# A first MoE tile of 288 tokens instead of 256, with its third piece transposed at the end of attention

## The chip, the cores and the metric

The kernel runs on one core of a Trainium2 chip. The metric is the time of one execution on the device, in microseconds (us). The kernel before takes 747.06 us, the median of three runs (746.73 to 747.48).

The engines are TensorE (PE: matmul and transpose, with its weight loads as PEld), VectorE (DVE), ScalarE (ACT), GpSimd (POOL) and SyncE (SP, which issues DMAs). Each runs its own instructions in order; they meet through semaphores. PE writes into PSUM, from which DVE and ACT take the results away.

## The reference

Three layers on 4 batches of 576 tokens, all in fp32: attention with a threshold on the scores (8 heads of 64), a mixture of 8 experts (512 to 1024 and back) in which a token keeps the expert of the token before it when its local gate is at least one half, and a second mixture of 4 attention experts, two for each token.

```python
scores = scale * np.matmul(q, k.transpose(0, 1, 3, 2))
thresh = np.max(scores, axis=-1, keepdims=True) - tau
scores = np.where(scores >= thresh, scores, -1000000000.0)
attn = np.exp(scores - np.max(scores, axis=-1, keepdims=True))
...
for b in range(B):
    prev_e = -1
    for s in range(S):
        fresh_e = int(np.argmax(logits[b, s]))
        e = fresh_e if s == 0 or local_gate[b, s] < 0.5 else (prev_e if prev_e >= 0 else fresh_e)
        prev_e = e
        ...
        h = np.maximum(x[b, s] @ w1[e], 0.0)
        out[b, s] = p[e] * (h @ w2[e])
...
for e in range(E):          # second mixture: 4 experts, top 2
    ...
    ye = a @ v @ wo[e]
```

## The kernel before

Products in fp32 are made of a high and a low half: three matmuls (high by high, high by low, low by high) take the place of one. A "split" makes the halves: the high half is a rounded copy (usually on ACT), the low half the difference (on DVE or POOL).

**Attention** (`stage1`, to about 281 us) goes through 16 pairs of heads, p = 0 to 15, each with nine tiles of scores. A score tile S (L246 to L251) takes one of three PSUM buffers in a ring; DVE takes the row maxima (L257), ACT the exponentials (L267), DVE the thresholding (L280, which reads S again and so sets that buffer free), and PE transposes the result (L293, X) and multiplies by v (L336, Y). When a pair is finished its rows are transposed on PE (L371; for the last pair's first half into a buffer of the score ring, S), ACT copies them (xraw), DVE takes the reciprocal of the sums (L363, rc, from input that POOL collects, L357 to L360), and POOL normalises (L396). The order is written out by hand: the table `W` and the numbers beside it give each step a time in units of a score tile, and steps are put down in the order of these numbers. The queries and keys of the next pair are split meanwhile, low halves on POOL (L204, L209).

**Early routing** (`Route.early`) runs inside the last pairs, by the times in `EARLY`. It routes batches 0 to 2, finds the fullest expert, and gives each of its tokens a position: `ranks` (L665) and `place` (L700) bring rank and position to `sle`, and POOL turns them into a column and a place within it (`column`, L707 to L718). One-hot matrices `ln` (L723, six on POOL at a time, and on DVE) and a product (L731, `invert`) turn that into token lists `inv`, 128 tokens to a column.

**The MoE stage** cuts the tokens of an expert into tiles of two kinds: P with 256 tokens (2 columns of `inv`), and L with 352 (3 columns; the first L, number 0, has `NL0` = 288, two chunks of 128 and one of 32). `SEQ` is the order of the tiles. Tile 0 belongs to the fullest expert of batches 0 to 2. Its tokens are gathered during the last pair of attention (`rows0`, at time `R0`, an indirect DMA on POOL, L1778), transposed on PE into score buffers (`tx0`, L1797, at the times `TX0`, by `xt.spare`), and split into xTPh (ACT, L1802) and xTPl (DVE, L1803). The halves of its expert's weights are split in the same stretch (`split0`, at the times `S0`: L924 to L927).

The rest of routing (`Route.main`, about 284 to 318 us) needs the logits of the last pair, and is a chain of small steps across PE, ACT and DVE. Tile 0 fills PE meanwhile: `start` cuts its work into pieces (first layer `h_mm`, L1054, in PSUM banks "acc"; second layer `y_mm`, L1083, in banks "py"), `FILL` says how many pieces stand between two steps of routing, and the evacuation of a bank (`hT_ev`: relu on ACT, L1043, low half on DVE, L1046) is put into `M.late` and taken out at set places. After routing the pieces that are left stand ahead of and between the transposes of tile 1 (`tx`, L1012), by `LEFT`. From about 320 us the other tiles follow one another, first layer and second layer, and then the second mixture.

In a chunk of 64 tokens or fewer ("packed"), high and low half lie side by side in `hT`, so that one matmul takes both, and `y_ev` adds the two results.

## Time and profile before

| | before |
|---|---|
| time, median of 3 | 747.06 us (746.73 to 747.48) |
| profiled execution | 748.55 us |
| its span | 746.8 us |
| PE busy | 722.0 us, 97% |
| DVE busy | 544.8 us, 73% |
| ACT busy | 490.7 us, 66% |
| POOL busy | 285.6 us, 38% |

The rows come from one execution taken by the profiler. Its time stands beside its span, the time from its first to its last instruction. In a timeline row stand the start, the duration, the engine, the line of the program, the operation, out<-in by the program's names, their sizes and the count; in brackets, how long the engine was idle before it and what released it. Neighbouring instructions of one line stand in one row. Matmuls overlap, so the duration of a matmul is longer than its distance from the next.

### The profile page before, as it was taken

The numbers are of one execution on the slowest core, as the hardware profiler recorded it, in microseconds if no ns is written. First come the engines' busy times: TensorE is split into PE (matmuls) and PEld (weight loads), VectorE is DVE, ScalarE is ACT, GpSimd is POOL, SyncE is SP. The second block draws the span as 40 slices with busy tenths as digits, with TensorE's granted clock in tenths as the row PEclk, the third lists the DMA queues.
The fourth block names the chain that finished last, engine by engine and source line by source line (L and its number), as shares of the span: only waits on it lengthen the run. The fifth ranks groups of instructions, "written<-read, shape, count | busy, mean of one in ns | idle before, by whom it ended". The sixth has DMA issues, their size and how long they took to land.

```text
span 746.8 us, 14233 instructions
## 1 busy us (share of the span) xinstructions
PE 722.0 (97%) x5063; PEld 611.4 (82%) x5063; DVE 544.8 (73%) x1427; ACT 490.7 (66%) x1026; POOL 285.6 (38%) x442
## 2 busy tenths in 40 slices
PE   5999999999999998999999999999998999999996
PEld 4887887888887777798889899989788888888874
DVE  7998999899988987725574475554269888878780
ACT  5888887888887784224565465444256887777883
POOL 6888888878777891300110110000356000000000
PEclk9999999999999999999999999999999999999999
DMA  8439444443332430295755656601333000100103
GB/s 281 149 116 315 147 124 139 137 156 120 122 126 66 185 119 18 87 372 179 253 204 206 240 184 211 237 1 53 95 86 99 2 16 1 43 15 29 44 29 104
DMA packets 37409, 95.40 MB, mean 128 GB/s; under 512 B 4337, under 2 KB 14833, under 8 KB 33233
## 3 DMA queue, kind: packets, MB, share of 16 engines
q1 hardware_dynamic: 30960, 73.62, 28.7%
q0 software_dynamic: 5360, 19.34, 8.3%
q10 hardware_dynamic: 1008, 1.44, 0.6%
q8 instruction: 42, 0.69, 0.4%
q14 instruction: 39, 0.31, 0.1%
HBM read 75.58 MB, written 18.81 MB: 126 GB/s over the span
## 4 chain that ended last, share of the span: by engine, by line
PE 84%; DVE 7%; ACT 4%; DMA 2%; issue 1%; POOL 1%; ACTq 0%; DVEq 0%; POOLq 0%
PE py L1083 16%; PE acc L1054 15%; PE Y L336 10%; PE S L246 9%; PE X L293 8%; PE AV L1647 4%; PE X L1596 3%; PE Y L371 2%; PE S L251 2%; PE S L1526 1%; PE px L1012 1%; PE S L1527 1%; PE misc L1446 1%; PE misc L1678 1%; PE misc L1677 1%
## 5 line engine op out<-in xcount | busy, mean ns | idle before, releaser
L280 DVE SCALAR_TENSOR_TENSOR P<-S,nm,E 128x576 f32<-128x576 f32 x144 | 116.3, 815 | 10.2 <-ACT E L267 4.5
L257 DVE TENSOR_REDUCE nm<-S 128x1 f32<-128x576 f32 x144 | 105.9, 754 | 17.6 <-PE S L246 16.8
L1083 PE MATMUL py<-w2h,hT 128*128 128x512 f32 (+2 forms) x344 | 114.8, 400 | 0.0
L267 ACT ACTIVATE E<-S,nm 128x576 f32<-128x576 f32 x144 | 104.1, 747 | 7.1 <-DVE nm L257 6.5
L246 PE MATMUL S<-KK,QS 128*128 128x288 f32 x256 | 84.0, 343 | 7.3 <-DVE QS L219 5.3
L293 PE MATMUL X<-cst,P 128*128 128x128 f32 x576 | 87.1, 278 | 1.4 <-ACT PT L304 0.7
L1778 POOL DMA_INDIRECT xg<-x_dram,inv x22 | 23.6, 1074 | 163.8 <-PE px L1012 128.2
L293 PEld LDWEIGHTS X<-cst,P 128*128 128x128 f32 x576 | 67.0, 142 | 16.1 <-issue 7.5
L304 ACT ACTIVATE PT<-X 128x512 f32<-128x512 f32 x128 | 75.8, 605 | 3.9 <-PE X L293 1.1
L1054 PE MATMUL acc<-xTh,w1h 128*128 128x256 f32 (+2 forms) x256 | 76.4, 299 | 0.0
L1054 PE MATMUL acc<-xTl,w1h 128*128 128x256 f32 (+2 forms) x256 | 76.0, 297 | 0.0
L1054 PE MATMUL acc<-xTh,w1l 128*128 128x256 f32 (+2 forms) x256 | 75.9, 297 | 0.0
L1083 PEld LDWEIGHTS py<-w2h,hT 128*128 128x128 f32 (+2 forms) x344 | 63.0, 183 | 15.4
L246 PE MATMUL S<-KL,QS 128*128 128x288 f32 x256 | 73.3, 300 | 0.3 <-DVE KL L201 0.3
L1083 PE MATMUL py<-w2l,hT 128*128 128x512 f32 (+2 forms) x176 | 69.4, 394 | 0.0
L336 PE MATMUL Y<-PT,v 128*64 128x320 f32 (+1 forms) x512 | 69.1, 412 | 0.2 <-ACT G L604 0.2
L1046 DVE SCALAR_TENSOR_TENSOR hT<-acc,hT 128x352 fp32r<-128x352 f32 (+3 forms) x60 | 30.4, 519 | 44.9 <-ACT hT L1043 44.9
L1043 ACT ACTIVATE hT<-acc 128x352 fp32r<-128x352 f32 (+2 forms) x52 | 26.2, 508 | 55.6 <-PE acc L1054 51.7
L246 PEld LDWEIGHTS S<-KK,QS 128*128 128x128 f32 x256 | 49.6, 194 | 8.8 <-ACT KK L192 5.2
L336 PEld LDWEIGHTS Y<-PT,v 128*64 128x64 f32 x512 | 33.9, 136 | 24.4 <-issue 4.8
L1847 POOL DMA_INDIRECT raw<-yg,slot x18 | 17.6, 980 | 86.8 <-DMA yg<-y 62.0
L246 PEld LDWEIGHTS S<-KL,QS 128*128 128x128 f32 x256 | 49.9, 195 | 0.6 <-DVE KL L201 0.6
(397 smaller groups left out, 1921.4 us busy)
## 6 DMA issues: line engine op xcount, KB each, us to landing
raw<-in_w_dram SPq DMA_DIRECT2D x32, 1024.0 KB, 5.4
kraw<-in_kT_dram SPq DMA_DIRECT2D x15, 608.0 KB, 4.1
QS<-in_qT_dram POOLq DMA_DIRECT2D x15, 576.0 KB, 4.1
v<-in_vp_dram SPq DMA_DIRECT2D x16, 320.0 KB, 3.0
yg<-y SPq DMA_DIRECT2D x17, 256.0 KB, 4.9
qraw<-in_qx_dram SPq DMA_DIRECT2D x15, 288.0 KB, 2.8
x_dram<-xr SPq DMA_DIRECT2D x16, 256.0 KB, 2.4
yg<-raw SPq DMA_DIRECT2D x1, 3072.0 KB, 12.9
```

The costliest lines, as they stand in the source:

```text
L246: nc.tensor.matmul(o, QS[p % NQ][:, a, cs], k[i][:, sl(576 * a)], start=(n == 0), stop=(n == 1))
L257: nc.vector.tensor_reduce(nm[:, 0:1], t[:, :, :288], axis=AX.XY, op=ALU.min)
L267: nc.scalar.activation(e, t[:, :, :288], AF.Exp, scale=-1.0, bias=nm[:, 0:1])
L280: nc.vector.scalar_tensor_tensor(PP[p, c][:, S * a:S * a + S].rearrange("p (h n) -> p h n", h=2), t[:, :, :288], nm[:, 1:2], e, op0=ALU.is ...
L293: nc.tensor.transpose(x[:, 128 * kc:128 * kc + 128], pp[:, o:o + 128], ident)
L304: nc.scalar.activation(PT[p, h][:, a, :, f:f + 128], x.rearrange("p (k q) -> p k q", k=4), AF.Copy)
L336: nc.tensor.matmul(out, l, r, start=s, stop=e, skip_group_check=True)
L1043: nc.scalar.activation(h[..., 0:w], p, AF.Relu)
L1046: nc.vector.scalar_tensor_tensor(h[..., low(t, c)], p[..., c], 0.0, h[..., c].bitcast(F32), op0=ALU.max, op1=ALU.subtract)
L1054: nc.tensor.matmul(o, a[:, fs], x[:, k, 0:w], start=(first and n == 0), stop=(k == 3 and n == 2), skip_group_check=True)
L1083: nc.tensor.matmul(ys[t][u][0:m], hT[t][i][:, f, k], w[:, 512 * f:512 * f + 512], start=(i == 0 and f == 0 and n == 0), stop=(i == 3 and f ...
L1647: nc.tensor.matmul(o[half(a), f:NH[h]], l, r, start=(k == 0), stop=(k == (1, 4)[h]), skip_group_check=True)
```

## The change

- Tile 0 becomes the 288-token tile and tile 1 a 256-token tile (`SEQ`). `rows0` gathers three pieces, the third of 32 tokens in a buffer of `qraw`; there are three transposes `tx0`, the last with 32 rows.
- The times `TX0`, `recip` and `S0` change: the copies and subtractions of the transposed rows stand ahead of the last pair's reciprocal, and the split of the first w2 chunk behind it.
- `column` now holds the arithmetic on the ranks too, which stood in `ranks` before: a token whose position is 288 or more gets its column from its rank less 288 (`NL0`).
- `start` takes one bank for each 288 columns, four banks ("py", "py", "acc", "acc") in turn, in pieces of six matmuls; a packed chunk of tile 0 follows at the end. `FILL` and `LEFT` change with the number of pieces (36 instead of 32).
- `hT` keeps the low half at a fixed offset, and POOL copies the packed chunk's low half beside its high half.
- The list `inv` has the columns of tile 0 at its end (last three instead of first two), so `main` writes 31 columns instead of 32, and `n0` has a sixth value.

```diff
-            T = dict(W, row=(11.3, 14.36), rev=(11.7, 14.7), recip=10.6, tpm=(8.79, 11.25), pmev=(9.07, 11.66))
+            T = dict(W, row=(11.3, 14.36), rev=(11.7, 14.7), recip=11.69, tpm=(8.79, 11.25), pmev=(9.07, 11.66))
...
     def rows0():
-        return P1.tile([128, 2, DM], F32, name="xg0", tag="P", bufs=5)
+        t = P1.tile([128, 2, DM], F32, name="xg0", tag="P", bufs=5)
+        return t[:, 0], t[:, 1], P1.tile([128, S], F32, name="qraw", bufs=2)[0:NL0 - 256, 0:DM]
...
-            q, one = self.rq, 1.5 * 2.0 ** 23
-            gp.tensor_scalar(q, sl[:, 0], -63.5, 1.0 / 128.0, op0=ALU.add, op1=ALU.mult)
-            gp.tensor_scalar(q, q, one, 1.0, op0=ALU.add, op1=ALU.mult)
-            gp.tensor_scalar(q, q, -one, 1.0, op0=ALU.add, op1=ALU.mult)
-            gp.tensor_scalar(self.place, q, -128.0, 1.0, op0=ALU.mult, op1=ALU.mult)
-            gp.tensor_tensor(self.place, self.place, sl[:, 0], op=ALU.add)
...
-            v.tensor_scalar(self.n0[:, 0:1], ti[:, 1:2], 256.0, t[:, 2:3], op0=ALU.min, op1=ALU.mult)
-            v.tensor_scalar(self.n0[:, 1:2], t[:, 2:3], NL0 - float(NL), NL - 511.0, op0=ALU.mult, op1=ALU.add)
+            v.tensor_scalar(self.n0[:, 0:1], ti[:, 1:2], float(NL0), t[:, 2:3], op0=ALU.min, op1=ALU.mult)
+            v.tensor_scalar(self.n0[:, 1:2], t[:, 2:3], NP0 - float(NL), NL - 511.0, op0=ALU.mult, op1=ALU.add)
...
+            v.tensor_scalar(self.n0[:, 5:6], t[:, 2:3], 3.0 - NCOL, NCOL - 3.0, op0=ALU.mult, op1=ALU.add)
...
         def column(*_):
-            sl, rq = T["sl"][:, 1], self.rq
-            f = T["f"] = E.tile([128, 4, 5, B], F32, name="fe")
+            sl, q, place, one = T["sl"][:, 1], self.rq, self.place, 1.5 * 2.0 ** 23
+            f = T["f"] = X.tile([128, 5, 5, B], F32, name="fe")
+            g = f[:, 4]
+            for i in (3, 0, 1, 2):
+                gp.tensor_scalar(f[:, i], sl, float(min(128 * i, NL0)), 1.0, op0=ALU.is_ge, op1=ALU.mult)
+                if i == 3:
+                    gp.tensor_scalar(g, f[:, 3], -float(NL0), 1.0, op0=ALU.mult, op1=ALU.mult)
+                    gp.tensor_tensor(g, g, T["sl"][:, 0], op=ALU.add)
+                    gp.tensor_scalar(q, g, -63.5, 1.0 / 128.0, op0=ALU.add, op1=ALU.mult)
+                    gp.tensor_scalar(q, q, one, 1.0, op0=ALU.add, op1=ALU.mult)
+                    gp.tensor_scalar(q, q, -one, 1.0, op0=ALU.add, op1=ALU.mult)
+                    gp.tensor_scalar(place, q, -128.0, 1.0, op0=ALU.mult, op1=ALU.mult)
+                    gp.tensor_tensor(place, place, g, op=ALU.add)
+            r2 = T["r2"] = X.tile([128, 5, B, 3], F16, name="r2e")
             for i in range(3):
-                gp.tensor_scalar(f[:, i], sl, 128.0 * i, 1.0, op0=ALU.is_ge, op1=ALU.mult)
-            r2 = T["r2"] = E.tile([128, 5, B, 2], F16, name="r2e")
-            for i in range(2):
                 gp.tensor_tensor(r2[:, :, :, i], f[:, i], f[:, i + 1], op=ALU.subtract)
-            gp.tensor_scalar(f[:, 3], f[:, 0], -2.0, 1.0, op0=ALU.mult, op1=ALU.mult)
-            gp.tensor_tensor(rq, rq, f[:, 3], op=ALU.add)
-            gp.tensor_scalar(f[:, 3], rq, 0.0, -128.0, op0=ALU.is_lt, op1=ALU.mult)
-            gp.tensor_tensor(rq, rq, f[:, 3], op=ALU.add)
-
-            gp.tensor_scalar(f[:, 3], f[:, 2], -1.0, 1.0, op0=ALU.mult, op1=ALU.add)
-            gp.tensor_tensor(self.s0.rearrange("p (j b) -> p j b", b=B), sl, f[:, 3], op=ALU.mult)
+            gp.tensor_tensor(f[:, 0], f[:, 0], f[:, 3], op=ALU.subtract)
+            gp.tensor_scalar(g, f[:, 0], -128.0, 1.0, op0=ALU.mult, op1=ALU.mult)
+            gp.tensor_tensor(q, q, g, op=ALU.add)
+            gp.tensor_scalar(g, sl, 128.0 * (NCOL - 3), 1.0, op0=ALU.add, op1=ALU.mult)
+            gp.tensor_tensor(self.s0.rearrange("p (j b) -> p j b", b=B), g, f[:, 0], op=ALU.mult)
...
-                mm(pi[:, 0:2], self.ln[:, j, b], T["r2"][:, j, b], start=(k == 0), stop=(k == 14))
-            return lambda: v.tensor_scalar(self.inv[:, 0:2], pi[:, 0:2], MID, None, op0=ALU.add)
-
-        return [copies, *self.choose_steps(slice(0, 3), gp), rows("A", 1), rows("G", 0), rest, flat, scan(0), scan(1), counted, turn,
+                mm(pi[:, 0:3], self.ln[:, j, b], T["r2"][:, j, b], start=(k == 0), stop=(k == 14))
+            return lambda: v.tensor_scalar(self.inv[:, NCOL - 3:], pi[:, 0:3], MID, None, op0=ALU.add)
...
-        NC = NCOL - 2
+        NC = NCOL - 3
...
-SEQ = [("P", 0), ("L", 0), ("P", 1), ("P", 2), ("L", 1), ("P", 3), ("P", 4), ("L", 2), ("L", 3)]
+SEQ = [("L", 0), ("P", 0), ("P", 1), ("P", 2), ("L", 1), ("P", 3), ("P", 4), ("L", 2), ("L", 3)]
...
-        p = bank("py" if (t, i) == (1, 1) else "px")
+        p = bank("px")
...
+        w = width(t)
+        hh, hl = (hT[t][i][:, n:, o:o + w] if w == 256 else hT[t][i][:, n, o:o + w] for o in (0, NL))
         p = p[:, 0:512].rearrange("p (f t) -> p f t", f=2) if w == 256 else p[:, 0:w]
-        nc.scalar.activation(h[..., 0:w], p, AF.Relu)
-        for c in (slice(0, w - m), slice(w - m, w)):
-            if c.stop > c.start:
-                nc.vector.scalar_tensor_tensor(h[..., low(t, c)], p[..., c], 0.0, h[..., c].bitcast(F32), op0=ALU.max, op1=ALU.subtract)
+        nc.scalar.activation(hh, p, AF.Relu)
+        nc.vector.scalar_tensor_tensor(hl, p, 0.0, hh.bitcast(F32), op0=ALU.max, op1=ALU.subtract)
+        c = chunks(t)[-1]
+        m = c.stop - c.start
+        if m <= 64 and n:
+            q = hT[t][i]
+            nc.gpsimd.tensor_copy(q[:, :, w:w + m], q[:, :, NL + c.start:NL + c.stop].bitcast(F32))
...
     def start():
         hT[0] = []
+        done = [0]
+        def ev(p, i, f):
+            done[0] += 1
+            hT_ev(0, p, i, f)
         for i in range(4):
-            p = P1.tile([128, 512], F32, name="acc", bufs=2)
-            for k in range(4):
-                for f in range(2):
-                    h_mm(0, p[:, 256 * f:256 * f + 256], 2 * i + f, k, k == 0 and f == 0)
-                if k == 3:
-                    M.late.append(lambda p=p, i=i: hT_ev(0, p, i, 0))
-                yield
+            for f in range(2):
+                if len(M.late) > 3:
+                    M.late.pop(0)()
+                p = PY.tile([128, 512], F32, name="py", bufs=2) if i % 2 == 0 else P1.tile([128, 512], F32, name="acc", bufs=2)
+                for h in range(2):
+                    for k in (2 * h, 2 * h + 1):
+                        h_mm(0, p[:, 0:NL0], 2 * i + f, k, k == 0)
+                    if h:
+                        M.late.append(lambda p=p, i=i, f=f: ev(p, i, f))
+                    yield
+        while done[0] < 6:
+            M.late.pop(0)()
         ys[0] = [bank("py") for _ in range(2)]
         for i in range(4):
+            while done[0] < 2 * i + 2:
+                M.late.pop(0)()
             for u in range(2):
                 for f in range(2):
                     y_mm(0, i, u, f)
                     if i == 3 and f == 1:
                         M.late.append(lambda u=u: y_ev(0, u))
                     yield
+        assert P2
+        ys[0].append(bank("py"))
+        for i in range(4):
+            for f in range(2):
+                y_mm(0, i, 2, f)
+            if i == 3:
+                M.late.append(lambda: y_ev(0, 2))
+            yield
...
-    left = 32
+    left = 36
...
-FILL = (3, 1, 4, 2, 1, 1, 3, 2, 1, 1)
+FILL = (3, 1, 4, 2, 1, 1, 3, 2, 1, 2)
...
-TX0 = ((145.6, 146.72), (145.7, 146.74))
-S0 = ((138.5, 140), (140.3, 142), (144.7, 145.3), (144.95, 145.35), (147.5, None), (146.71, 146.9))
-LEFT = (13, 9, 4)
+TX0 = ((145.6, 146.665), (145.7, 146.67), (145.71, 146.672))
+S0 = ((138.5, 140), (140.3, 142), (144.7, 145.3), (144.95, 145.35), (146.68, None), (146.71, 146.9))
+LEFT = (15, 10)
...
-                for i in range(2):
-                    gather(M.x0[:, i], x_dram[0:3], rt.inv[:, i:i + 1])
-                M.xT0 = tuple(E.tile([128, 4, 256], F32R, name="xTP" + q) for q in "hl")
+                for x, c in zip(M.x0, cols("L", 0)):
+                    m = x.shape[0]
+                    gather(x, x_dram[0:3], rt.inv[0:m, c:c + 1])
+                M.xT0 = tuple(E.tile([128, 4, NL0], F32R, name="xTP" + q) for q in "hl")
             def tx0(i):
                 def f(xt, _):
-                    p = xt.spare()
+                    p, m = xt.spare(), M.x0[i].shape[0]
                     for c in range(4):
-                        nc.tensor.transpose(p[:, 128 * c:128 * c + 128], M.x0[:, i, 128 * c:128 * c + 128], K["ident"])
-                    h, l = (t[:, :, 128 * i:128 * i + 128] for t in M.xT0)
-                    pv = p.rearrange("p (c t) -> p c t", c=4)
+                        nc.tensor.transpose(p[:, m * c:m * c + m], M.x0[i][:, 128 * c:128 * c + 128], K["ident"][0:m, 0:m])
+                    h, l = (t[:, :, 128 * i:128 * i + m] for t in M.xT0)
+                    pv = p[:, 0:4 * m].rearrange("p (c t) -> p c t", c=4)
...
-                for c in cols("L", 0):
+                for c in cols("P", 0):
```

POOL, from the split of the last pair's queries (L209, QS) to the first one-hot group (`ln`). `sle` holds ranks and positions, `fe`, `rq` and `place` the arithmetic on them, `r2e` the column masks. Before:

```order
L209 TENSOR_TENSOR QS_112<-qraw,QS_112 64x576
L667 TENSOR_SCALAR rq<-sle 128x20
L668 TENSOR_SCALAR rq<-rq 128x20
L669 TENSOR_SCALAR rq<-rq 128x20
L670 TENSOR_SCALAR place<-rq 128x20
L671 TENSOR_TENSOR place<-place,sle 128x20
L209 TENSOR_TENSOR QS_112<-qraw,QS_112 64x576
L223 CAST QM_122<-QS_112 128x64 x2
L707 TENSOR_SCALAR fe<-sle 128x20 x3
L710 TENSOR_TENSOR r2e<-fe 128x20 x2
L712 TENSOR_SCALAR fe<-fe 128x20
```

And with the change:

```order
L209 TENSOR_TENSOR QS_112<-qraw,QS_112 64x576 x2
L223 CAST QM_122<-QS_112 128x64 x2
L703 TENSOR_SCALAR fe<-sle 128x20
L705 TENSOR_SCALAR fe<-fe 128x20
L706 TENSOR_TENSOR fe<-fe,sle 128x20
L707 TENSOR_SCALAR rq<-fe 128x20
L708 TENSOR_SCALAR rq<-rq 128x20
L709 TENSOR_SCALAR rq<-rq 128x20
L710 TENSOR_SCALAR place<-rq 128x20
L711 TENSOR_TENSOR place<-place,fe 128x20
L703 TENSOR_SCALAR fe<-sle 128x20 x3
L714 TENSOR_TENSOR r2e<-fe 128x20 x3
```

The five operations that stood between the two query splits now stand behind both and behind the first comparison of the positions; from there to the one-hot group there were eleven operations and are nineteen.

PE, at the end of the last pair. The numbers behind a name tell one buffer from another; S are buffers of the score ring, X transposes of scores, Y_4215 and Y_4228 the last attention product. Before:

```order
L1797 MATMUL S_4165<-cst_62,xg0_4053 128x128 x4
L293 MATMUL X_4170<-cst_62,P_4093 128x128 x4
L1797 MATMUL S_4175<-cst_62,xg0_4053 128x128 x4
L293 MATMUL X_4184<-cst_62,P_4146 128x128 x4
L317 MATMUL Y_4189<-cst_62,P_3994 128x128
L317 MATMUL Y_4189<-cst_62,P_4093 128x128
L320 MATMUL Y_4189<-iq_115 128x64
L371 MATMUL S_4193<-iq_115,XT1_105 128x146 x2
L336 MATMUL Y_4215<-PT1_4070,v_3191 64x320 x8
L336 MATMUL Y_4215<-PM1_4197,v_3191 64x320 x2
L1054 MATMUL acc_4271<-xTPh_4056,w1h_3966 128x256
```

And with the change:

```order
L1823 MATMUL S_4170<-cst_62,xg0_4056 128x128 x4
L293 MATMUL X_4175<-cst_62,P_4098 128x128 x4
L1823 MATMUL S_4180<-cst_62,xg0_4056 128x128 x4
L1823 MATMUL S_4185<-cst_62,qraw_4057 128x32 x4
L293 MATMUL X_4194<-cst_62,P_4151 128x128 x4
L317 MATMUL Y_4199<-cst_62,P_3997 128x128
L317 MATMUL Y_4199<-cst_62,P_4098 128x128
L320 MATMUL Y_4199<-iq_115 128x64
L371 MATMUL S_4203<-iq_115,XT1_105 128x146 x2
L336 MATMUL Y_4228<-PT1_4075,v_3191 64x320 x8
L336 MATMUL Y_4228<-PM1_4207,v_3191 64x320 x2
L1057 MATMUL py_4284<-xTPh_4061,w1h_3969 128x288
```

The third transpose takes a score buffer of its own, so four S buffers in a row are taken where there were three, and the first matmul of tile 0 writes into a bank "py" instead of "acc".

DVE, at the end of the last pair: the split of tile 0's weights (w1, w2), the transposed rows' low half (xTPl), and the last pair's reciprocal (rc) with a small product of it. Before:

```order
L924 CAST w1h<-raw_72 128x1024
L927 TENSOR_TENSOR w1l<-raw_72,w1h 128x1024 x2
L363 RECIPROCAL rc<-rc 128x10
L387 TENSOR_TENSOR lg<-S,rc 128x36
L924 CAST w2h<-raw_74 128x1024
L1803 TENSOR_TENSOR xTPl<-S,xTPh 128x4x128 x2
L927 TENSOR_TENSOR w2l<-raw_74,w2h 128x1024
```

And with the change:

```order
L929 CAST w1h<-raw_72 128x1024
L932 TENSOR_TENSOR w1l<-raw_72,w1h 128x1024 x2
L1829 TENSOR_TENSOR xTPl<-S,xTPh 128x4x128 x2
L1829 TENSOR_TENSOR xTPl<-S,xTPh 128x4x32
L363 RECIPROCAL rc<-rc 128x10
L387 TENSOR_TENSOR lg<-S,rc 128x36
L929 CAST w2h<-raw_74 128x1024
L932 TENSOR_TENSOR w2l<-raw_74,w2h 128x1024
```

The subtractions of the transposed rows, now three, move ahead of the reciprocal and of the w2 cast.

## Rows read from the trace of the kernel before

**Rows 1.** The page's busy line: time, share of the span, instructions of each engine.

```profile
PE 722.0 (97%) x5063; PEld 611.4 (82%) x5063; DVE 544.8 (73%) x1427; ACT 490.7 (66%) x1026; POOL 285.6 (38%) x442
```

**Rows 2.** Stretches: length, then busy PE, PEld, DVE, ACT, POOL; clock, DMA.

```profile
200.00:300.00 100.00, 95.76 (x773) 77.32 (x772) 86.15 (x236) 74.08 (x149) 66.56 (x108) 1.00 0.30 100
300.00:320.00 20.00, 18.99 (x119) 14.91 (x119) 12.21 (x47) 5.89 (x10) 7.42 (x7) 1.00 0.40 113
320.00:330.00 10.00, 10.00 (x78) 10.00 (x77) 3.13 (x12) 2.88 (x7) 0.00 (x0) 1.00 1.00 415
```

**Rows 3.** Waits of PE, 200 to 325 us: total, times, longest.

```profile
PE acc L1054 <- DVE xTPl L1803: 1.3, 1, 1.3
PE py L1012 <- issue: 0.5, 1, 0.5
...
PE prest L765 <- ACT hT L1043: 0.5, 1, 0.5
PE acc L1054 <- DVE rk L825: 0.3, 1, 0.3
...
PE acc L1054 <- DVE ti L795: 0.3, 1, 0.3
...
PE prest L765 <- DVE q L864: 0.2, 1, 0.2
```

**Rows 4.** Timeline of POOL, 253 to 270 us.

```profile
253.84 0.79 POOL L707 TENSOR_SCALAR fe<-sle 128x20 f32<-128x20 f32 x3 [0.38 <-DVE sle L700]
...
256.78 4.70 POOL L723 TENSOR_SCALAR ln<-io,place,cst 128x128 f16<-128x128 f16 x6
...
264.17 0.21 POOL L360 TENSOR_SCALAR rc<-RS 128x10 f32<-128x10 f32 x1
264.48 4.71 POOL L723 TENSOR_SCALAR ln<-io,place,cst 128x128 f16<-128x128 f16 x6
```

**Rows 5.** Timeline of DVE, 264 to 268 us.

```profile
264.41 0.22 DVE L363 RECIPROCAL rc<-rc 128x10 f32<-128x10 f32 x1
...
267.30 0.82 DVE L280 SCALAR_TENSOR_TENSOR P<-S,nm,E 128x576 f32<-128x576 f32 x1
```

**Rows 6.** Timeline of PE, 269 to 270 us.

```profile
269.18 0.39 PE L246 MATMUL S<-KK,QS 128*128 128x288 f32 x1
...
269.80 0.53 PE L731 MATMUL Y<-r2e,ln 128*128 128x2 f16 x15
```

**Rows 7.** Timeline of PE, 280 to 286 us.

```profile
280.50 0.72 PE L371 MATMUL S<-iq,XT 128*128 128x146 f32 x4
...
285.33 0.36 PE L1054 MATMUL acc<-xTPh,w1h 128*128 128x256 f32 x1 [1.27 <-DVE xTPl L1803]
```

**Rows 8.** Timeline of all engines, 280 to 284 us, ACT and DVE.

```profile
280.77 0.43 ACT L325 ACTIVATE PM<-Y 128x320 f32<-128x320 f32 x1
...
282.33 0.22 DVE L363 RECIPROCAL rc<-rc 128x10 f32<-128x10 f32 x1 [1.60 <-POOL rc L360]
...
283.27 1.08 ACT L1802 ACTIVATE xTPh<-S 128x512 fp32r<-128x512 f32 x2
...
283.89 1.29 DVE L1803 TENSOR_TENSOR xTPl<-S,xTPh 128x512 fp32r<-128x512 f32 x2 [0.45 <-ACT xTPh L1802]
```

**Rows 9.** Timeline of POOL, 273 to 281 us.

```profile
273.08 0.96 POOL L1778 DMA_INDIRECT xg<-x_dram,inv  x1 [0.30 <-issue]
...
277.61 3.32 POOL L396 TENSOR_TENSOR lg<-xraw,rc 128x90 f32<-128x90 f32 x1
```

**Rows 10.** The chain that ended last: start, length, engine, matmuls of one first layer.

```profile
318.34 12.73 PE acc L1054 x96
```

**Rows 11.** Groups by form: busy us, mean ns of one, idle before and its releaser.

```profile
L396 POOL TENSOR_TENSOR lg<-xraw,rc 128x90 f32<-128x90 f32 x15 | 8.1, 539 | 0.0
...
L1046 DVE SCALAR_TENSOR_TENSOR hT<-acc,hT 128x512 fp32r<-128x512 f32 x20 | 13.7, 688 | 16.0 <-ACT hT L1043 16.0
L1046 DVE SCALAR_TENSOR_TENSOR hT<-acc,hT 128x352 fp32r<-128x352 f32 x24 | 12.5, 523 | 17.0 <-ACT hT L1043 17.0
```

More of the change, by code (lines that the diff above doesn't have):

```diff
@@ L519, in __init__ @@
         self.fr = X.tile([128, 5, B], F32, name="fr")
-        self.eq = X.tile([128, 5, B, 8], F32, name="eq")
         self.U = X.tile([128, 2, 5, B, 8], BF16, name="U")
@@ L524, in __init__ @@
         self.e0 = C.tile([32, 1], I32, name="e0")
-        self.n0 = X.tile([32, 5], F32, name="n0")
+        self.n0 = X.tile([32, 6], F32, name="n0")
         self.s0 = X.tile([128, 20], F32, name="s0")
@@ L542, in bc @@
             return ap[:, :, bs].unsqueeze(3).to_broadcast([128, 5, n, 8])
-        l8, q = self.L[:, :, bs, 0:8], self.eq[:, :, bs]
+        l8, q = self.L[:, :, bs, 0:8], pool.tile([128, 5, n, 8], F32, name="eq", **kw)
         w8 = K["w8"].unsqueeze(1).unsqueeze(1).to_broadcast([128, 5, n, 8])
@@ L619, in flat @@
             gp.memset(aux[:, 128:256], 1.0)
-            sl = T["sl"] = E.tile([128, 2, 5, B], F32, name="sle")
+            sl = T["sl"] = X.tile([128, 2, 5, B], F32, name="sle")
             gp.memset(sl, -1.0)
@@ L625, in counted @@
             OB = T["OB"] = self.scratch("OB", BF16, 640)
-            n = T["n"] = E.tile([32, 1], F32, name="ne")
+            n = T["n"] = X.tile([32, 1], F32, name="ne")
             gp.memset(OB[rs, S:640], 0.0)
@@ L652, in out @@
             def out():
-                sf = T["sf"] = E.tile([32, 4], BF16, name="sf")
+                sf = T["sf"] = X.tile([32, 4], BF16, name="sf")
                 v.tensor_scalar(t[:, 16:17], sm[0:32, 129:130], 16.0, K["prefrow"][0:32], op0=ALU.mult, op1=ALU.add)
@@ L730, in invert @@
                 j, b = divmod(k, 3)
-                mm(pi[:, 0:2], self.ln[:, j, b], T["r2"][:, j, b], start=(k == 0), stop=(k == 14))
-            return lambda: v.tensor_scalar(self.inv[:, 0:2], pi[:, 0:2], MID, None, op0=ALU.add)
-        return [copies, *self.choose_steps(slice(0, 3), gp), rows("A", 1), rows("G", 0), rest, flat, scan(0), scan(1), counted, turn,
+                mm(pi[:, 0:3], self.ln[:, j, b], T["r2"][:, j, b], start=(k == 0), stop=(k == 14))
+            return lambda: v.tensor_scalar(self.inv[:, NCOL - 3:], pi[:, 0:3], MID, None, op0=ALU.add)
+        return [copies, *self.choose_steps(slice(0, 3), E, gp, tag="w1h", bufs=4), rows("A", 1), rows("G", 0), rest, flat, scan(0), scan(1), counted, turn,
                 count, ranks, most, taken, place, column, *[hot(k) for k in range(5)], invert]
@@ L750, in main @@
         fill(0)
-        for f in self.choose_steps(slice(3, 4)):
+        for f in self.choose_steps(slice(3, 4), W):
             f()
@@ L784, in main @@
         v.tensor_tensor_scan(R, K["ones"][:32, 0:1].to_broadcast([32, S]), O[:, :S], 0.0, op0=ALU.mult, op1=ALU.add)
-        self.M.late.pop(0)()
+        if self.M.late:
+            self.M.late.pop(0)()
         n = R[:, S - 1:S]
@@ L852, in main @@
             j, b = divmod(i, B)
-            small(pi, ln3[:, j] if b == 3 else self.ln[:, j, b], r1[:, i], stop=(n == 19))
-        v.tensor_scalar(inv[:, 2:], pi, MID, None, op0=ALU.add)
+            r = slice(0, 128 if j < 4 else S - 512)
+            small(pi, ln3[r, j] if b == 3 else self.ln[r, j, b], r1[r, i], stop=(n == 19))
+        v.tensor_scalar(inv[:, :NC], pi, MID, None, op0=ALU.add)
         first()
@@ L1025, in moe_ops, with packed @@
     hT = {}
-    def packed(t):
-        c = chunks(t)[-1]
-        return c.stop - c.start if c.stop - c.start <= 64 else 0
-    def low(t, c):
-        w, m = width(t), packed(t)
-        o = w if m and c.stop == w else w + m + c.start
-        return slice(o, o + c.stop - c.start)
+    def packed(t, u):
+        c = chunks(t)[u]
+        return c.stop - c.start <= 64
     def hT_ev(t, p, i, n):
@@ L1076, in y_mm @@
         c = chunks(t)[u]
-        l = low(t, c)
-        ops = [(c, wh), (c, wl), (l, wh)]
-        if l.start == c.stop and packed(t):
-            ops = [(slice(c.start, l.stop), wh), (c, wl)]
-        for n, (k, w) in enumerate(ops):
-            m = k.stop - k.start
-            nc.tensor.matmul(ys[t][u][0:m], hT[t][i][:, f, k], w[:, 512 * f:512 * f + 512], start=(i == 0 and f == 0 and n == 0),
+        m = c.stop - c.start
+        h = hT[t][i][:, f]
+        hh, hl = h[:, c], h[:, NL + c.start:NL + c.stop]
+        ops = [(hh, wh, m), (hh, wl, m), (hl, wh, m)]
+        if packed(t, u):
+            ops = [(h[:, c.start:c.start + 2 * m], wh, 2 * m), (hh, wl, m)]
+        for n, (h, w, m) in enumerate(ops):
+            nc.tensor.matmul(ys[t][u][0:m], h, w[:, 512 * f:512 * f + 512], start=(i == 0 and f == 0 and n == 0),
                              stop=(i == 3 and f == 1 and n == len(ops) - 1), skip_group_check=True)
@@ L1101, in y_ev @@
         ny[0] += 1
-        if s.stop == width(t) and packed(t):
+        if packed(t, u):
             lo = W.tile([128, DM], F32, name="ylo", tag="xg", bufs=4)
@@ L1211, in moe @@
     ws, erow, fetch, fetch3, xscale = M.ws, M.erow, M.fetch, M.fetch3, M.xscale
-    for i in range(3):
+    for i in range(2):
         while left > LEFT[i]:
```

15 lines of the change are left out of this document (7 added, 8 removed).

## The prediction

> **What bounds the kernel now.** I read the page's busy line first: TensorE (PE) is busy 722.0 us, 97% of the span [rows 1]. The table of stretches says where the rest is. In the body of the MoE stage PE is never idle (10.00 of 10 us), while the 120 us in which attention ends and the tokens are routed lose some 5 us [rows 2]. So work that only moves from one MoE tile to another is worth nothing by itself; what can change is PE's waiting between 250 and 318 us. Those waits are few: 1.3 us for the low half of tile 0's transposed rows (xTPl), 0.5 ahead of the small products of the scan R (L765, put down to ACT's hT), 0.3 twice for a PSUM bank that VectorE (DVE) has not emptied, 0.2 for q, and 0.5 ahead of the second transpose of tile 1 [rows 3]. Together 3.1 us, 0.4% of the time: this is all that a longer tile 0 can win.
>
> **The change part by part.** Sums are made against the profiled execution: 748.55 us, of which 746.8 is the span and 1.75 lies around it. It ran 1.5 us above the median of the timed runs, 747.06, and I carry differences over to that median.
>
> *Work moved.* Tile 0 goes from 256 to 288 columns and tile 1 from 288 to 256, each with 96 matmuls of the first layer; the packed third chunk (16 matmuls of the second layer, 4 small transposes, an evacuation) moves with the 32 columns. A 288-column matmul has a pitch of 12.73/96 = 0.133 us [rows 10]; by the ratio of columns one of 256 has 0.118. So tile 0 gains 1.4 us there and tile 1 loses 1.4; chunk and transposes cancel too. Zero.
>
> *POOL's column arithmetic.* Before, five operations on the ranks stand ahead of the last query split, and eleven behind the wait for the positions; these eleven fill 253.84 to 256.78, a spacing of 0.27 us [rows 4]. Now all nineteen stand behind that wait. Eight more at 0.27 are 2.1 us, and GpSimd (POOL) has no idle time from there to the reciprocal's input at 264.17 and the last one-hot group at 264.48 [rows 4].
>
> What waits for it: DVE's reciprocal ran at 264.41, right behind POOL's 264.17 + 0.21, so it now runs near 266.5. Behind it in DVE's order stands the thresholding (start 267.30, 0.82 us) that ends a score tile, now done near 270.3 [rows 5]. PE's scores at 269.18 take that tile's buffer, one of three in a ring, and so wait 1.1 us. The inversion matmuls at 269.80 need POOL's last one-hot, which ended at 264.48 + 4.71 and now ends at 271.3: another 0.2 to 0.4 [rows 4, 6]. I take +1.3 us. Bounds: 0, if slack between the engines takes it all, to 2.1.
>
> *A fourth user of the score buffers.* The three transposes of tile 0 and the first row product of the last pair (L371, S) now take four buffers out of the ring of three. The row product must wait until ScalarE (ACT) has copied the first transpose and DVE has subtracted it. ACT gets there behind PM (280.77, 0.43 us); its copy leads the subtraction by 0.62 us, and one subtraction is half of 1.29 [rows 8]. That gives 280.77 + 0.43 + 0.62 + 0.65 = 282.5 where the product ran at 280.50 [rows 7], and the attention product is queued behind it: +2.0 us of PE. Bounds: 1.6 (ACT's operations overlap a little, two copies taking 1.08) to 2.4.
>
> *The wait that goes.* ACT and DVE now do the transposes ahead of the row product's copy and of the reciprocal, so the rows are ready while PE is at the attention product. The 1.27 us at 285.33 go [rows 7]. What is late next is the bank of tile 0's first matmul: in the new order that matmul waits for ACT, whose copy of the row product waits for the last pair's reciprocal, and that for POOL. POOL is 2.1 us later and has a third gather, 0.30 + 0.96 more. Its normalisation then falls under DVE's cast and subtractions, as a small product of it did before: 3.32 us where its kind has a mean of 0.54, up to 280.9 [rows 9, 11]. DVE's part of that now ends 1.5 later, near 282.5; the normalisation and the sums behind it take some 3 us, from the 1.4 us between 280.9 and the reciprocal at 282.33 and the products that now come after the block too [rows 8]. So the reciprocal has its input near 285.8 and the copy ends near 286.9. PE comes there at 285.33 − 1.27 + 1.3 + 2.0 + 0.35 (the third transpose) = 287.7: hidden, with 0.8 us to spare.
>
> The 3.32 us are one collision. The Trainium skill, "SBUF — State Buffer", Who interferes with whom, says that a DVE instruction with two SBUF inputs or in a two-port mode shuts out GpSimd's reads, and that one with a single SBUF input does not. The collision agrees with the first half (the subtractions of weights have both inputs in SBUF). By the second half the transposes' subtractions, which read PSUM, would leave POOL alone.
>
> *Routing window.* Tile 0 uses four PSUM banks where it had two, so the waits of 0.3 at ti and rk go. Pieces of six matmuls are 0.8 us instead of 0.7, seven of them ahead of R, and cover its 0.5. New: four bank evacuations instead of two lie in DVE's chain ahead of the inversion's input; by the rows for 512 and 352 columns one of 288 takes 0.46 us, so 1.8 instead of 1.4, of which I give PE 0.2 [rows 11]. The first matmul of the second layer takes a bank that DVE empties only behind q, so that 0.7 stands where q's wait had 0.2. The second transpose of tile 1 waits for the single px buffer, 0.4 instead of 0.5. Old 1.8, new 1.3: −0.5 us. Bounds −1.8 (all go) to +0.5.
>
> *Covered edits.* The seventh operation on n0 and the low halves that POOL copies lie where DVE and POOL wait for PE: nothing; uncovered, 0.2 us each. The weights of tile 2 are asked for some 3 us earlier, ahead of a PE that doesn't wait for them: nothing. The small matmuls with three columns instead of two and 31 instead of 32: nothing.
>
> Sum: +1.3 + 2.0 − 1.3 − 0.5 = +1.5 us, so 748.5 us.
>
> **The rivals.**
> *The window pays it back.* DVE and PE run loosely enough near 264 to 270 that POOL's 2.1 us reach PE as nothing, the buffer wait is at its lower bound, and all 1.8 us of the window's waits go: 1.6 − 1.3 − 1.8 = −1.5, 745.5 us. For it: longer pieces and more banks are just what the waits at R, ti and rk lack. Against: the reciprocal at 264.41 had no slack against POOL, and three buffers leave PE about 1 us.
>
> *POOL becomes the gate.* POOL's normalisation is shut out through the transposes' subtractions as well (1.3 us), or its w1l split before it is, and the reciprocal's input lands after 286.6. From there on each us is one of PE's, since the bank of tile 0's first matmul hangs on it. Price 0.5 to 1.5 beside the sum: 749.0 to 750.0 us, slower. For it: the collision before cost 2.8 us [rows 9]. Against: that one had a DVE operation of another kind beside it.
>
> *The buffer wait doesn't come*, because the row product gets a buffer that is free earlier: −0.5 us, 746.5, no change. The order in which buffers are taken speaks against it.
>
> **How the numbers follow.** A difference under 0.2%, 1.5 us, cannot be told from none here, and the forecast sits on that edge. It has 0.55, with its own range of +0.3 to +2.5 us and three fifths of it inside the bound. POOL as the gate has 0.15, all slower. The window that pays back has 0.2, taken as faster: the trace before can't show how the engines settle after a shift. No buffer wait has 0.1, no change. Slower: 0.55 × 0.4 + 0.15 = 0.37; faster 0.2; no change 0.43. The range takes in the better part of both sides, 745.4 to 750.0.
>
> **What would show it.** In the profile after: POOL's first one-hot group starts near 259 instead of 256.78; DVE's reciprocal waits 2 us for POOL near 264; PE waits about 1 us ahead of a score matmul near 269; PE stands 2 us ahead of L371 S with DVE's xTPl as releaser; the 1.3 us ahead of the first-layer matmul are gone, and the waits at ti and rk too; one of about 0.7 appears ahead of the first second-layer matmul. I am wrong if PE has no wait ahead of the row product, if the score matmuls near 269 don't wait, or if the stretch from the end of the last attention product to the start of tile 2 shrinks by more than 3 us.

## The result, and the profile after

| | before | after |
|---|---|---|
| median of 5 runs | 747.06 us (746.67 to 747.48) | 757.34 us (756.31 to 759.21) |
| ratio | | 1.0138, 95% interval 1.0127 to 1.0149 |
| profiled execution, its span | 748.55, 746.8 us | 757.32, 755.5 us |

The changed kernel is 1.4% slower, and the forecast of 748.5 us (745.4 to 750.0) is wrong by 9 us. The page's busy line of the kernel after, against [rows 1]:

```profile
PE 726.3 (96%) x5063; PEld 614.6 (81%) x5063; DVE 543.4 (72%) x1420; ACT 489.4 (65%) x1026; POOL 285.8 (38%) x449
```

PE has the same 5063 instructions and is busy 4.3 us longer, so some of them ran slower; the other 4.4 us of the longer span are idle time. The spans of the two profiled executions differ by 8.7 us and the medians by 10.3, since the profiled execution before ran 1.5 above its median; the account below goes by the profiles. The waits of PE from 200 to 345 us (total, times, longest) say where, against [rows 3]:

```profile
PE py L1087 <- DVE hT L1044: 4.8, 2, 4.4
PE S L371 <- DVE xTPl L1829: 2.1, 1, 2.1
PE S L246 <- DVE P L280: 0.6, 1, 0.6
...
PE X L293 <- DVE inv L734: 0.5, 1, 0.5
PE px L1017 <- DVE xTl L1023: 0.3, 1, 0.3
```

The second, third and fourth row shown are at places that the prediction named. The first is not in it: 4.4 us ahead of tile 1's second layer. Its row in the timeline of all engines, and what stands before it on VectorE and in SyncE's queue (start, length, engine, instruction, in brackets the idle time and its releaser):

```profile
320.15 0.15 DVE L914 COPY erow<-er 1x23 int32<-1x23 int32 x1
...
321.30 3.98 SPq L985 DMA_DIRECT2D raw<-in_w_dram  x6
...
325.40 17.24 SPq L1115 DMA_DIRECT2D yg<-y  x3
...
341.62 0.68 DVE L1109 TENSOR_TENSOR y<-py,ylo 32x512 f32<-32x512 f32 x1 [21.31 <-DMA yg<-y]
...
342.95 1.22 PE L1087 MATMUL py<-w2h,hT 128*128 128x512 f32 x2 [4.42 <-DVE hT L1044]
```

Read backwards: PE waits for VectorE's evacuations of tile 1 (hT); these stand behind the sum that evacuates tile 0's third chunk (L1109); and that has waited 21.3 us for a store. `y_ev` takes the buffers of its results in turn from two, "xTPh" and "xTPl". The third result of tile 0 takes the first one's, and may not write before the first result is stored. That store stands in SyncE's queue behind six weight loads of 1 MB each. Before, the stores landed as late, 17.6 us behind their issue. But tile 0 had two results, and the third came from tile 1, at 348.91 us, 27.7 us after the stores were issued:

```profile
321.19 0.91 SPq L1111 DMA_DIRECT2D yg<-y  x2
...
348.91 0.68 DVE L1105 TENSOR_TENSOR y<-py,ylo 32x512 f32<-32x512 f32 x1 [5.58 <-issue]
```

The clock shows in stretches around the two long waits: length, then busy PE, PEld, DVE, ACT, POOL, the granted clock (1.00 is 2.4 GHz, 0.50 is 1.2 GHz), DMA:

```profile
284.00:286.00 2.00, 0.81 (x3) 0.82 (x4) 2.00 (x5) 1.87 (x4) 0.96 (x3) 0.70 0.00 0
286.00:288.00 2.00, 2.00 (x9) 0.94 (x9) 1.45 (x4) 0.41 (x1) 0.00 (x0) 0.50 0.00 0
...
290.00:292.00 2.00, 2.00 (x16) 1.81 (x15) 0.20 (x1) 0.44 (x1) 0.39 (x3) 1.00 0.00 0
...
344.00:346.00 2.00, 2.00 (x6) 1.61 (x5) 0.69 (x2) 0.00 (x0) 0.00 (x0) 0.50 0.47 137
```

Behind the wait of 2.1 us and behind that of 4.4 us PE runs at half speed for about three us. The chain of waits prices the second: ten matmuls take 4.07 us where twelve of the same kind take 2.79 a little later, 0.2325 each; 4.07 − 10 × 0.2325 = 1.75 us.

```profile
342.95 4.07 PE py L1087 x10
347.02 0.44 PE px L1017 x4
347.45 2.79 PE py L1087 x12
```

The starts of five pieces of PE's work, from the timelines, make the account:

| PE starts | before | after | later by |
|---|---|---|---|
| scores of the second-last buffer | 269.18 | 270.44 | 1.26 |
| first transpose of tile 0's rows | 278.27 | 280.22 | 1.95 |
| last pair's row product | 280.50 | 285.19 | 4.69 |
| tile 0's first matmul | 285.33 | 290.14 | 4.81 |
| tile 2's first matmul | 346.61 | 356.07 | 9.46 |

Between the row product and tile 0's first matmul the 1.27 us for xTPl are gone, but the work takes 4.95 us instead of 3.56: 1.4 us of half speed. The row product and the attention product after, and the latter before (the former took 0.72 there, [rows 7]):

```profile
285.19 1.34 PE L371 MATMUL S<-iq,XT 128*128 128x146 f32 x4 [2.10 <-DVE xTPl L1829]
286.46 3.21 PE L336 MATMUL Y<-PT,v 128*64 128x320 f32 x16
```

```profile
281.14 2.38 PE L336 MATMUL Y<-PT,v 128*64 128x320 f32 x16
```

From there to tile 2 the kernel loses 4.65: 4.42 of the wait, 1.75 of the clock, less a rest of 1.5, put down to the routing window.

### The profile page after: what moved, and what is told of

Same layout as the page of the kernel before. It is cut to its first block, busy times and chain, and to the rows that moved or that the text cites. A ratio compares the mean times of both kernels' runs of the same rounds, so it can differ in the third digit from the quotient of the medians.

```text
span 755.5 us, 14231 instructions
## 1 busy us (share of the span) xinstructions
PE 726.3 (96%) x5063; PEld 614.6 (81%) x5063; DVE 543.4 (72%) x1420; ACT 489.4 (65%) x1026; POOL 285.8 (38%) x449
## 4 chain that ended last, share of the span: by engine, by line
PE 80%; DVE 7%; DMA 5%; ACT 3%; POOL 2%; issue 2%; SPq 1%; ACTq 0%; POOLq 0%; DVEq 0%
PE py L1087 14%; PE acc L1057 13%; PE Y L336 10%; PE S L246 8%; PE X L293 7%; PE AV L1672 4%; PE X L1621 3%; PE Y L371 2%; DMA yg<-y 2%; PE S L251 2%; PE misc L1434 1%; PE S L1552 1%; DMA QS<-in_qT_dram 1%; PE S L1551 1%; PE misc L1436 1%
## 5 line engine op out<-in xcount | busy, mean ns | idle before, releaser
L1057 PE MATMUL acc<-xTl,w1h 128*128 128x256 f32 (+1 forms) x256 | 76.1, 297 | 0.0
L1057 PE MATMUL acc<-xTh,w1l 128*128 128x256 f32 (+1 forms) x256 | 75.9, 297 | 0.0
L1057 PE MATMUL acc<-xTh,w1h 128*128 128x256 f32 (+1 forms) x256 | 75.8, 296 | 0.0
L1043 ACT ACTIVATE hT<-acc 128x352 fp32r<-128x352 f32 (+2 forms) x48 | 24.6, 515 | 54.2 <-PE acc L1057 54.1
L1044 DVE SCALAR_TENSOR_TENSOR hT<-acc,hT 128x352 fp32r<-128x352 f32 (+2 forms) x48 | 27.7, 584 | 36.7 <-ACT hT L1043 36.7
L1873 POOL DMA_INDIRECT raw<-yg,slot x18 | 17.6, 977 | 85.9 <-DMA yg<-y 62.1
```

What stands on the lines that cost most here:

```text
L1043: nc.scalar.activation(hh, p, AF.Relu)
L1044: nc.vector.scalar_tensor_tensor(hl, p, 0.0, hh.bitcast(F32), op0=ALU.max, op1=ALU.subtract)
L1057: nc.tensor.matmul(o, a[:, fs], x[:, k, 0:w], start=(first and n == 0), stop=(k == 3 and n == 2), skip_group_check=True)
```

## The experiments

Each kernel was compared with the kernel before on the same chip; 0.0013 of a ratio is 1 us. Theory A: the buffer of tile 0's third result, held by a store that is queued behind the loads, makes the block at tile 1. Theory B: the fourth score buffer makes the wait ahead of the row product, and the clock behind it. Theory C: GpSimd's longer column arithmetic makes the waits near 270 us. The rivals stand in the expectations.

**The block at tile 1.** Two edits take the wait away in different places: another buffer, and another order in the queue.

```diff
# own buffer: the sum is written over its low part
+        own = t == 0 and packed(t, u)
...
+            if own:
+                y = lo
```

> The changed kernel, with the third result of tile 0 (32 tokens) added up in place, in the buffer that already holds its low part, instead of in the buffer of tile 0's first result. Theory A (buffer): VectorE's sum waited 21.3 us for the store of the first result, which stands in SyncE's queue behind six weight loads of 1 MB, and the evacuations of tile 1 stood behind it; so PE's 4.4 us ahead of tile 1's second layer go, and the 1.7 us that its clock at half speed cost behind them: 757.3 - 6.1 = 751.2 us (750.5 to 752). Rival: tile 1, now 256 tokens, is simply too short for its evacuations, and the wait stays under another name: 757.3.

```diff
# stores first
-    for _ in range(6):
-        load()
     for _ in pieces:
         M.flush()
+        left -= 1
+        if left == 3:
+            for _ in range(6):
+                load()
```

> The changed kernel, with the six weight loads put behind the stores of tile 0's first two results in SyncE's order. Theory A, and in it that the queue is at fault and not the buffer as such: the store lands within 3 us of its issue, VectorE's sum runs near 327.5, and the same 6.1 us go: 751.2 us. The loads start 3 to 4 us later and end near 342, where the first split of tile 2's weights is due near 341: 0 to 2 us may come back, up to 753. Rival (the buffer waits for something else than the queue): 757.3.

Own buffer: 752.33 us, ratio 1.0060 (1.0047 to 1.0073), so 5.8 us of the 10.3 are gone. Stores first: 750.71 us, ratio 1.0039 (1.0025 to 1.0052), 7.4 us. In both the 4.4 us are gone, and VectorE's sum runs at 328.73 and 327.59 instead of 341.62. The rival, a tile 1 that is too short, falls. The DMA issues (KB each, median us from issue to landing), after and then with the stores first, show that it is the loads issued ahead of the store:

```profile
raw<-in_w_dram SPq DMA_DIRECT2D x6, 1024.0 KB, 10.7
yg<-y SPq DMA_DIRECT2D x2, 256.0 KB, 16.2
```

```profile
raw<-in_w_dram SPq DMA_DIRECT2D x7, 1024.0 KB, 10.1
yg<-y SPq DMA_DIRECT2D x2, 256.0 KB, 2.0
```

The same store lands in 2.0 us ahead of the loads and in 16.2 behind them. The Trainium skill, "DMA: Bandwidth & Descriptors", Queues, rings and completion order, says that SyncE's transfers go into one queue row of its own, whose rings are worked through in order; the trace agrees. A store from another engine's queue was not tried, so it is not shown whether the order in SyncE's queue alone holds it, or the loads would hold it from any queue. By the traces the two edits should be worth the same. In the one with its own buffer the half speed behind the row product lasted longer, some five us, with tile 0's first matmul at 291.44 instead of 290.30; that is 1.1 of the 1.6 us between them. Why it lasted longer is open.

**The fourth score buffer.**

```diff
-    def spare():
-        return PSS.tile([128, 2, 512], F32, name="S", tag="S", bufs=3)[:, 0]
+    def spare(both=False):
+        t = PSS.tile([128, 2, 512], F32, name="S", tag="S", bufs=3)
+        return t if both else t[:, 0]
...
+                    if i == 1:
+                        M.x0p = xt.spare(True)
+                    p = M.x0p[:, i - 1] if i else xt.spare()
```

> The changed kernel, with the 32-row transposes written into the second bank of the score buffer that the second transposes use, so that three score buffers are taken and not four. Theory B: the 2.1 us that PE waits ahead of the last pair's row product go, and with them the half clock from 285 to 288.5 (some 1.9 us): 757.3 - 4.0 = 753.3 us. Rival: the wait only moves to tile 0's first matmul, whose bank hangs on ScalarE's copy of the row product and that on the reciprocal at 285.85; then PE waits about 1.2 us there: 754.5. If the block of 6.1 us at tile 1 takes it up (it is set by a DMA): smaller by up to 2.

754.70 us, ratio 1.0096 (1.0083 to 1.0109): 3.1 us less. PE no longer waits ahead of the row product. The wait moves in part to tile 0's first matmul, whose bank waits for ScalarE's copy of the row product, as the rival said. The block at tile 1 is still there, with 3.29 us. The timeline of PE in this kernel:

```profile
284.01 0.72 PE L372 MATMUL S<-iq,XT 128*128 128x146 f32 x4
...
288.31 0.40 PE L1058 MATMUL py<-xTPh,w1h 128*128 128x288 f32 x1 [0.73 <-ACT xraw L390]
...
339.89 0.72 PE L1088 MATMUL py<-w2h,hT 128*128 128x512 f32 x2 [3.29 <-DVE hT L1045]
```

**Both edits together** (own buffer, third transposes beside the second).

> The changed kernel with both edits, own buffer for tile 0's third result and the 32-row transposes beside the second ones. If the two costs are separate they add: 757.3 - 6.1 - 4.0 = 747.2 us, no change against before. If they hide behind one another: 749 to 750.

748.91 us, ratio 1.0017 (1.0008 to 1.0026): 9.0 us less than the changed kernel; the parts sum to 8.9, so the two costs are separate, as far as intervals of about 1 us on each part can tell. Tile 2 starts at 346.73, within 0.2 us of before. The edit has a cost of its own. ScalarE's three copies of the transposed rows in the changed kernel, and the third copy and subtraction in this one:

```profile
283.55 1.26 ACT L1828 ACTIVATE xTPh<-S 128x512 fp32r<-128x512 f32 x3
```

```profile
285.33 0.28 ACT L1836 ACTIVATE xTPh<-S 128x128 fp32r<-128x128 f32 x1 [1.13 <-DVE xTPl L1837]
...
285.64 0.29 DVE L1837 TENSOR_TENSOR xTPl<-S,xTPh 128x128 fp32r<-128x128 f32 x1 [0.34 <-ACT xTPh L1836]
```

Beside the second transposes, ScalarE's third copy waits for VectorE's subtraction of the second, and VectorE then stands idle for 0.34 us ahead of the reciprocal. Every later form of the changed kernel has these two waits.

**GpSimd's column operations.** What is left in that kernel are the waits of 0.6 and 0.5 us near 270, and 1.0 ahead of tile 0's first matmul. The first try moved nothing:

```diff
-            gp.tensor_tensor(f[:, 0], f[:, 0], f[:, 3], op=ALU.subtract)
...
+            def tail():
+                gp.tensor_tensor(f[:, 0], f[:, 0], f[:, 3], op=ALU.subtract)
...
+            self.tail = tail
...
+        self.tail()
         fill(0)
```

> Both edits of the kernel that ran at 748.9 us (own buffer for the third result, transposes beside one another), and of GpSimd's nineteen column operations the last five (the column numbers, which nothing needs before the rest of routing) put off to where GpSimd is idle, near 286 us. Theory C: these operations hold up GpSimd's chain by 5 x 0.27 = 1.35 us; with them gone PE's 0.62 us ahead of the scores and 0.48 us behind the inversion go, and the weight subtraction of GpSimd no longer meets VectorE's small sum (1.96 us where it took 0.32 before), so that part of the 1.0 us ahead of tile 0's first matmul goes too: 746.8 to 747.9 us, 747.3. Rival: VectorE is late by itself there, and GpSimd's lateness costs nothing: 748.9.

749.06 us, ratio 1.0021 (1.0011 to 1.0031), with the same waits. In its timeline the five operations stand at 261.66, directly behind the first one-hot group and still ahead of the reciprocal's input: the scheduler had moved them there. Two more kernels below (the reciprocal in its old place, and the stores first) are built on it. In the kernel before the same edit gave

> The kernel before, with the last six of its eleven column operations put off in the same way. PE had no wait there for GpSimd, so by theory C nothing is to be won: 747.1 us, within 0.5. Rival (GpSimd is the gate of this stretch in the kernel before too, and every operation counts): 6 x 0.27 = 1.6 us less, 745.5.

748.28 us, ratio 1.0012 (1.0002 to 1.0023), which says nothing on theory C for the same reason: there the operations stand at 259.88, behind the first one-hot group. Why it is 0.9 us slower is not shown. With the reciprocal and the w2 split back in their old place:

> The kernel with three edits (own buffer, transposes beside one another, column operations put off), and the reciprocal and the first w2 split in VectorE's order where the kernel before has them. If the moved reciprocal is what holds tile 0's bank, its wait goes and that for the transposed rows (1.3 us before) comes back in part: within 0.5 of the kernel with three edits. If the new order is worth the 1.3 us that the prediction gave it: 1.0 to 1.3 slower than that kernel, 748.5.

750.30 us, ratio 1.0032 (1.0021 to 1.0044), 0.8 us slower than the kernel with three edits, with intervals that overlap: the new order of ScalarE and VectorE may be worth something, but 1.3 is not shown. Its profiled execution had a clock of 0.83 from 270 to 280 us, that of the kernel with three edits 1.00, so the 0.8 may be partly that. And with the stores first in the place of the own buffer:

> The kernel with three edits, but with the stores ahead of the six weight loads in the place of the own buffer. Theory A: either takes the wait away, so the two agree within 0.5 us; if the stores are worth something by themselves (the loads that follow them cost nothing), 0.5 to 1 faster: 746.5.

749.47 us, ratio 1.0025 (1.0015 to 1.0035): the two ways agree here. That is 8.4 us less than the changed kernel, where the stores first (7.4) and the third transposes beside the second (3.1) sum to 10.5; so how far the parts add is known within some 2 us only. Then the same operations were given a time of their own in the event table:

```diff
-                count, ranks, most, taken, place, column, *[hot(k) for k in range(5)], invert]
+                count, ranks, most, taken, place, column, *[hot(k) for k in range(5)], invert, lambda *a: self.tail(*a)]
...
-         (129.25, 129.45), (129.5, 130.6), 130.65, 130.93, 144.9, (132, 132.36), 132.38, 133, 134.5, 136, 137.5, 139, (141.1, 141.4))
+         (129.25, 129.45), (129.5, 130.6), 130.65, 130.93, 144.9, (132, 132.36), 132.38, 133, 134.5, 136, 137.5, 139, (141.1, 141.4), 148)
```

> The kernel of 748.9 us (own buffer, transposes beside one another), with the last five of the nineteen column operations given a late time of their own, so that they stand behind the sums of the last pair in GpSimd's order (in the run before, the scheduler had drawn them forward to the first one-hot group, ahead of the reciprocal's input, and nothing moved). Theory C: the reciprocal's input comes 1.35 us earlier, VectorE's reciprocal near 265 instead of 266.3; PE's waits of 0.6 ahead of the scores and 0.5 behind the inversion go, and so does most of the 1.0 ahead of tile 0's first matmul: 747.0 to 747.8 on the scale of 748.9, and level with or under the kernel before. Rival (VectorE's own work gates this stretch): 748.9, with the same waits.

747.16 us, ratio 1.0004 (0.9995 to 1.0013): 1.0 us less than with both edits alone, and 1.3 less than with the first try, which had the same waits. VectorE's reciprocal after, and then here:

```profile
266.80 0.22 DVE L363 RECIPROCAL rc<-rc 128x10 f32<-128x10 f32 x1 [2.11 <-POOL rc L360]
```

```profile
264.88 0.22 DVE L364 RECIPROCAL rc<-rc 128x10 f32<-128x10 f32 x1 [0.77 <-POOL rc L361]
...
277.40 1.97 DVE L680 TENSOR_TENSOR n<-n 32x1 f32<-32x1 f32 x1
```

The wait for GpSimd is 1.34 us shorter, which is five operations at 0.27. PE's 0.6 us ahead of the scores are gone and 0.4 of the 0.5 behind the inversion stay. The 1.0 us ahead of tile 0's first matmul stay too, against the expectation. The kernel before with its six operations put off in this way:

> The kernel before, with the last six of its eleven column operations put off in the same way, behind the sums of the last pair. GpSimd's chain is 1.6 us shorter; PE waited for none of it in this stretch. Theory C: no change, 747.1 within 0.7. Rival (GpSimd sets the pace of the stretch in the kernel before as well): 1 to 1.6 us less.

747.51 us, ratio 1.0004 (0.9995 to 1.0013): no change, as theory C has it.

**A small sum of 2 us.** The row at 277.40 above is a sum of 32 values on VectorE.

```diff
-            v.tensor_tensor(self.n0[:, 1:2], self.n0[:, 1:2], self.n0[:, 0:1], op=ALU.add)
+            v.tensor_scalar(self.n0[:, 1:2], self.n0[:, 1:2], self.n0[:, 0:1], None, op0=ALU.add)
```

> The kernel of 747.16 us (own buffer, transposes beside one another, last five column operations late), with VectorE's sum of two values of n0 written as an addition of a scalar (one tensor in SBUF as input in place of two). The sum of 32 values took 1.97 us in that kernel, beside GpSimd's weight subtraction, and 0.32 in the kernel before; its neighbours with a scalar took 0.2 beside the same subtraction. Theory D (two SBUF inputs on VectorE wait for GpSimd's instruction to end): the operation takes about 0.2, VectorE's chain to the transposed rows is up to 1.7 us earlier, and PE's 1.0 us ahead of tile 0's first matmul go: 746.2 us. Rival (the instruction waits for something else, or GpSimd's sums then collide with VectorE's weight subtractions and the reciprocal comes no earlier): 747.2.

747.08 us, ratio 0.9996 (0.9987 to 1.0005). The timeline of GpSimd and VectorE there:

```profile
276.09 2.40 POOL L935 TENSOR_TENSOR w1l<-raw,w1h 128x1024 fp32r<-128x1024 f32 x1
...
277.77 0.20 DVE L680 TENSOR_SCALAR n<-n 32x1 f32<-32x1 f32 x1
...
278.15 2.12 DVE L932 CAST w1h<-raw 128x1024 fp32r<-128x1024 f32 x1
...
278.41 1.30 POOL L397 TENSOR_TENSOR xr<-xraw,rc 128x640 f32<-128x640 f32 x1
```

The sum takes 0.20 us, so theory D holds for it; but the cast behind it takes 2.12 where it took 0.67 before. The wait has only moved to another instruction, the reciprocal comes no earlier (284.50 instead of 284.40), and PE still waits 0.75 ahead of tile 0's first matmul. Both halves of the expectation, theory and rival, are true. The last kernel has ScalarE's copy ahead of the w2 split as well:

> The same, and ScalarE copies the last pair's row product ahead of the split of the first w2 chunk (1.06 us) instead of behind it. If the 1.0 us ahead of tile 0's first matmul hangs on this copy and the scalar sum alone does not free it, this does: 746.2 us where the other stays at 747.2; if the scalar sum frees it, the two agree within 0.3.

747.78 us, ratio 1.0005 (0.9996 to 1.0014): nothing won, PE's wait is 0.63. The copy had mostly been released late, not queued late: it starts at 285.40, right behind VectorE's product with the reciprocal (285.09, 0.20). No version beats the kernel before beyond its interval: with its three faults mended, the change is worth nothing that can be measured.

## Why the prediction was wrong

- *POOL's column arithmetic, +1.3 us: the mechanism right, the size low, within its bounds.* The reciprocal waits 2.11 us for GpSimd, the first one-hot group starts at 259.20, PE's scores near 269 are 1.26 us later. Behind the inversion PE waits 0.48 more, and tile 0's first transpose is 1.95 later. Putting off 1.35 us of that work gave 1.0 us back.
- *A fourth user of the score buffers, +2.0: the wait right, its price too small.* It measured 2.10 us with the releaser named. The step left out that PE's clock falls behind such a wait, another 1.4 us; the wait of 1.27 us in [rows 7] had shown nothing of the kind.
- *The wait that goes, −1.3: right.* The 1.27 us are gone. What was named as next, the bank that waits for ScalarE's copy, stood hidden behind the row product's wait, and came out with 0.6 to 1.0 us as soon as that was taken away (0.3 with the reciprocal in its old place). "Hidden, with 0.8 us to spare" was right only beside the other wait; and part of what came out belongs to the edit that took it away, whose 0.34 us lie ahead of the reciprocal.
- *The rival "POOL becomes the gate" did not come.* The reciprocal's input was ready at 285.11 and VectorE took it at 285.85, behind its own subtractions. Beside the subtractions of weights GpSimd's operations took 1.14 and 1.18 us where they took 0.28 and 0.18 before; beside those of the transposed rows one took 0.18:

```profile
282.02 2.51 DVE L932 TENSOR_TENSOR w1l<-raw,w1h 128x1024 fp32r<-128x1024 f32 x2
282.30 1.14 POOL L427 TENSOR_TENSOR L<-L,lg 128x45 f32<-128x45 f32 x1
283.39 1.18 POOL L357 COPY RS<-sM 64x1 f32<-64x1 f32 x1
284.46 1.47 DVE L1829 TENSOR_TENSOR xTPl<-S,xTPh 128x512 fp32r<-128x512 f32 x3
284.63 0.18 POOL L358 COPY RS<-sM 64x1 f32<-64x1 f32 x1
```

- *Routing window, −0.5: too small.* It gave 1.1 by the waits from 292 to 318 us (0.4 and 0.3 are left of 1.8), 1.5 as the rest of the starts on PE.
- *Work moved, "zero", with "the packed third chunk (16 matmuls of the second layer, 4 small transposes, an evacuation)": this step failed.* The matmuls do cancel. The evacuation does not: where it stands now, its buffer is released by a store behind 6 MB of loads. That is 4.4 us of wait and 1.75 of clock, 6.2 us by the trace, and 5.8 and 7.4 by the two edits that take it away. The rivals had GpSimd as a gate and the window, all before 318 us; none looked at the buffers of the results.
- *The weights of tile 2 "asked for some 3 us earlier": wrong.* The expert numbers came at 320.15 instead of 315.92, 4.2 us later, since the whole window started 4.8 later. It cost nothing: where the block was gone, tile 2 did not wait.

At the start of tile 2 the kernel is 9.46 us late. Without the block's 6.2 that is 3.3, where the prediction had a sum of 1.5; the clock behind the row product is 1.4 of the difference. The rest of the loss, the block, came from an edit that the prediction had cleared by counting instructions on PE.

The collision of [rows 9] was read from one side only. The Trainium skill, "SBUF — State Buffer", Who interferes with whom, says also that "Issue order, not op shape, decides who blocks". The runs agree: in the kernel with the late column operations GpSimd's normalisation starts 1.67 us later than before (278.06 instead of 276.39). There it was quick (0.36 us for the product that took 3.32), and VectorE's sum of 32 values, issued while GpSimd subtracted weights, waited instead, 1.97 us, to the end of the GpSimd instruction after that one.
